# Mish as one ScalarE function, with a new order of the whole program and casts spread over three engines

## The chip, the cores and the metric

The kernel runs on one core of one Trainium2 chip. The core has a matmul engine (TensorE, PE in the profile), three engines for elementwise work (VectorE, DVE; ScalarE, ACT; GpSimd, POOL), and one queue (SyncE, SP) that issues the DMAs here. Each engine takes its instructions in the order in which the program was written and waits on semaphores for the others. The metric is the device time of one execution in microseconds; the median of three runs before is 551.99 us (550.8 to 553.58).

## The reference

Two parts follow one another. The first is a gated linear recurrence (4 batches, 8 heads, 768 steps, head size 40), the second a feed-forward layer with Mish over 3072 tokens (320 to 2048 to 320). Everything is float32.

```python
for t in range(S):                                   # first part, per batch and head
    m_new = np.maximum(f_gate[:, :, t] + m, i_gate[:, :, t])
    f_stab = np.exp(f_gate[:, :, t] + m - m_new); i_stab = np.exp(i_gate[:, :, t] - m_new); m = m_new
    C = f_stab * C + i_stab * outer(v_t, k_t);  n = f_stab * n + i_stab * k_t
    y[:, :, t] = sigmoid(o_gate_t) * (C @ q_t) / np.maximum(np.abs(n . q_t), 1.0)

h = x @ w_in                                         # second part, x = y as 3072 x 320
sp = np.where(h > 20.0, h, np.log1p(np.exp(np.minimum(h, 20.0))))
g = h * np.tanh(sp)                                  # Mish
out = g @ w_out
```

The weights w_in and w_out come as float64 and are handed to the kernel as pairs of 32-bit words.

## The kernel before

The 3072 tokens are cut into 12 units of 256 tokens (u or n), each of two chunks (c) of 128. For each chunk the first part is done in matrix form: `scores` (q against k), `decay` (four Exp passes on ACT, one for each head), `causal` (the mask, on POOL), `pmul`, `intra` and `inter` (the two parts of the output), `state_mm` and `state` (the carried matrix), `denom`, the output gate in five steps `gate_o`, `gate_den`, `xmul`, and then the transpose `flip_mm` and its two halves `flip_hi` and `flip_lo`.

The second part goes in 96 slots: 12 units times 8 pairs of hidden blocks (p). To keep float32 exactness with a faster matmul type, each operand is split into a rounded high half and the rest. A slot is `mm1` (two halves j of 8 matmuls of 256 columns each, into a PSUM bank pair h, of which there are two), Mish, the split of the result into gh and gl, and `mm2` (two halves of 6 matmuls of 320 columns each, adding into acc). The tiles e, gh and gl have two buffers each.

Mish is h·(1 − 1/(0.5·(1+e^h)² + 0.5)), with e^h cut off so that it stays finite. That is six passes over a 128x512 tile and two more for the split:

| call | engine | what | line |
|---|---|---|---|
| mish_exp | ACT | Exp of h | L1503 |
| mish_min | DVE or POOL | cut at e^20 | L1507 |
| mish_rest 0, 1, 2 | ACT | Square, Ln, Exp | L1512, L1514, L1516 |
| mish_out 0 | DVE | (1 − e)·h, after which h is free | L1521 |
| mish_out 1 | DVE or ACT | gh, the rounded copy | L1196 (the helper `copy`) |
| mish_out 2 | DVE or POOL | gl = e − gh | L1528 |

All of ACT's functions in it lie in one table set, which is loaded once at the start (L1714).

The weights are converted in the kernel as well: 16 chunks (8 of w_in, 8 of w_out) are loaded, through three buffers, and go through `conv` in six steps: a scaling on ACT (L1228), three integer steps on DVE (L1230, L1232, L1234), the rounded half wih or woh (L1196, on ACT or DVE) and the rest wil or wol (L1238, on POOL or DVE). A slot p needs the conversion of its w_in chunk for mm1 and of its w_out chunk for mm2. Units 0 and 1 run their slots in alternating halves meanwhile, and their partial sums are put aside by `dump`. While weights and first inputs are loaded, 42 `warm` matmuls on zeros run on PE.

The order of the program is not that of the loops. Each call is entered by `at` with a time, and by `after` with the calls that must come before it; `emit` puts them in order of time under those needs. The times come from a table TIMES: a start for calls of the first units, an offset within the slot (of 4.4 us) for the others, and own times for the last two units. A table 'eng' in it names the engine of each cast, split and conversion. As every engine, and the SP queue too, runs in program order, this list sets what waits behind what on each.

Of the kernel before, what the change touches and what calls it, by code (L numbers as in the profile page):

```python
# [7 lines left out]
F32 = mybir.dt.float32  # L8
# [18 lines left out]
LAG = 2  # L27
KN = H * D
VN = H * D1
E20 = 485165195.40979  # L30
# [6 lines left out]
SLOT = 4.4  # L37
NB = NU
TIMES = {'mm1': [-0.149, 0.276],
 'mish_exp': -1.727,  # L40
 'mish_min': 0.556,
 'mish_rest': [0.925, -2.788, 0.213],
 'mish_out': [1.068, 1.915, -0.004],
 'mm2': [2.849, 0.289],
 'store': [2.139, 2.543],
 'decay': [[-2.011, -0.53], [1.29, 2.675]],
 'causal': [[1.179, 0.533], [0.229, 3.083]],
 'scores': [[1.493, 2.193], [2.16, 3.297]],
 'pmul': [[0.588, 2.056], [4.029, 4.412]],
 'gate_o': [[-0.073, 0.11, 0.23, 0.764, 2.964], [2.985, 3.425, 3.545, 2.599, 5.248]],  # L50
 'weigh_v': [1.002, 3.434],
 'state_mm': [1.553, 5.355],
 'state': [1.83, 4.829],
 'inter': [-0.408, 5.492],
 'intra': [[2.475, 3.282], [5.629, 5.791]],
 'denom': [3.216, 4.039],
 'gate_den': [2.212, 6.091],
 'xmul': [3.581, 6.08],
 'flip_mm': [4.447, 7.002],
 'flip_hi': [4.544, 6.181],  # L60
 'flip_lo': [4.602, 7.365],
 'load_raw': -7.874,
 'load_ea': -7.594,
 'load_kvo': [-3.832, -3.594],
 'set_abc': -4.191,
 'carry': -6.024,
 'make_qs': -5.899,
 'split_hi': [-5.402, -5.297],
 'split_lo': [-6.621, -3.312],
 'stack': -1.727,  # L70
 'xdup': [3.631, 6.13],
 'block1': 64.45,
 'eng': {'gate_o_0_0_0': 'S',
         'gate_o_0_1_0': 'S',
         'gate_o_1_0_0': 'S',
         'gate_o_1_1_0': 'S',
         'mish_out_0_0_1': 'V',
         'mish_out_0_0_2': 'G',
         'mish_out_0_1_1': 'V',
         'mish_out_0_1_2': 'G',  # L80
         'mish_out_0_2_1': 'V',
         'mish_out_0_2_2': 'G',
         'mish_out_0_3_1': 'S',
         'mish_out_0_3_2': 'G',
         'mish_out_0_4_1': 'S',
         'mish_out_0_4_2': 'G',
         'mish_out_0_5_1': 'V',
         'mish_out_0_5_2': 'G',
         'mish_out_0_6_1': 'V',
         'mish_out_0_6_2': 'G',  # L90
         'mish_out_0_7_1': 'V',
         'mish_out_0_7_2': 'V',
         'split_hi_2_0': 'V',
         'split_hi_2_1': 'V',
         'mish_min_0_0': 'V',
         'mish_min_0_1': 'G',
         'mish_min_0_2': 'G',
         'mish_min_0_3': 'G',
         'dump_0_0': 'V',
         'dump_0_1': 'V',  # L100
         'mish_min_1_0': 'V',
         'mish_out_1_0_1': 'V',
         'mish_out_1_0_2': 'G',
         'mish_min_1_1': 'V',
         'mish_out_1_1_1': 'S',
         'mish_out_1_1_2': 'G',
         'mish_min_1_2': 'V',
         'mish_out_1_2_1': 'S',
         'mish_out_1_2_2': 'G',
         'mish_min_1_3': 'V',  # L110
         'mish_out_1_3_1': 'V',
         'mish_out_1_3_2': 'G',
         'dump_1_0': 'S',
         'dump_1_1': 'S',
         'mish_min_0_4': 'V',
         'mish_min_0_5': 'G',
         'mish_min_0_6': 'V',
         'mish_min_0_7': 'V',
         'mish_min_1_4': 'G',
         'mish_out_1_4_1': 'V',  # L120
         'mish_out_1_4_2': 'G',
         'mish_min_1_5': 'V',
         'mish_out_1_5_1': 'V',
         'mish_out_1_5_2': 'V',
         'mish_min_1_6': 'G',
         'mish_out_1_6_1': 'S',
         'mish_out_1_6_2': 'G',
         'mish_min_1_7': 'V',
         'mish_out_1_7_1': 'V',
         'mish_out_1_7_2': 'G',  # L130
         'weigh_v_0_0': 'V',
         'gate_den_0_0': 'G',
# [1773 lines left out]
```

## Time and profile before

| | |
|---|---|
| median of three runs | 551.99 us |
| the profiled execution | 554.73 us |
| its span, first to last instruction | 553.0 us |
| mean granted TensorE clock | 0.944 |
| busy: PE, DVE, ACT, POOL | 507.7, 430.8, 358.3, 212.1 us |
| matmuls | 3714 |
| first matmul of mm1 | 46.8 us |
| last output copy begins | 549.9 us |

A busy engine is one with an instruction in flight. PE's matmuls are pipelined: while it is dense, the next one begins some 0.12 us after the last although each is shown as lasting about 0.3 us, so the count of matmuls in a stretch says more than the busy share. DVE, ACT and POOL take one instruction at a time, with a small overlap. Rows of groups give the busy sum, the mean time of one in ns, and the idle time of the engine just ahead of them with what ended it.

### The profile page before, as it was taken

What the parts mean: (1) busy time and instruction counts of PE and PEld (TensorE: products, weight loads), DVE (VectorE), ACT (ScalarE), POOL (GpSimd) and SP (SyncE); (2) the same over time, 40 slices, a digit from 0 to 9 for tenths busy, and PEclk for the clock granted to TensorE, in tenths of its full rate; (3) what the DMA queues carried; (4) which work ended last, traced back from release to release, by engine and by line L of the source; (5) the groups of instructions that cost most, each with busy time, mean ns of one, the idle gap of its engine ahead of it and who ended that gap; (6) DMA issues with size and microseconds to landing.
All of it is one profiled execution on the core that took longest, in us unless ns stands there. A gap on an engine that the chain in (4) does not pass through costs nothing.

```text
span 553.0 us, 10133 instructions
## 1 busy us (share of the span) xinstructions
PE 507.7 (92%) x3714; PEld 490.9 (89%) x3714; DVE 430.8 (78%) x814; ACT 358.3 (65%) x718; POOL 212.1 (38%) x194
## 2 busy tenths in 40 slices
PE   6999877789999988998998998998998998999997
PEld 5998766778999988998998998997988997999997
DVE  7858999999977669759669769769669769778654
ACT  3636864766774756765766756756756756775774
POOL 4726986775651215116225215215215215212010
PEclk9558977997999998999998999999999999999999
DMA  7884853565434552453562552552551561510000
GB/s 204 262 250 149 268 196 105 165 194 154 143 90 137 165 148 82 148 135 111 160 166 70 158 154 81 163 162 71 166 169 58 172 182 41 170 35 1 2 25 24
DMA packets 40778, 73.72 MB, mean 133 GB/s; under 512 B 3048, under 2 KB 22440, under 8 KB 40568
## 3 DMA queue, kind: packets, MB, share of 16 engines
q1 hardware_dynamic: 40728, 73.07, 43.8%
q8 instruction: 29, 0.48, 0.4%
q14 instruction: 21, 0.17, 0.1%
HBM read 49.27 MB, written 4.13 MB: 97 GB/s over the span
## 4 chain that ended last, share of the span: by engine, by line
PE 44%; DVE 19%; DMA 15%; SPq 9%; issue 5%; ACT 4%; POOL 3%; DVEq 0%; POOLq 0%; ACTq 0%
PE h L1499 15%; SPq L1300 8%; DMA out_dram<-ob 7%; PE acc L1545 6%; PE acc L1543 5%; PE acc L1544 5%; DMA stk<-raw 5%; PE y L1386 4%; DVE gh L1196 3%; DMA raw<-in_qk_dram 3%; DVE e L1507 3%; PE s L1335 2%; PE warm L1786 2%; DVE wr L1232 2%; PE m L1397 2%
## 5 line engine op out<-in xcount | busy, mean ns | idle before, releaser
L1499 PE MATMUL h<-xh,wih 128*128 128x256 f32 x576 | 164.2, 291 | 7.1 <-DVE e L1521 7.0
L1499 PE MATMUL h<-xh,wil 128*128 128x256 f32 x576 | 154.8, 284 | 1.0 <-DVE wil L1238 1.0
L1543 PE MATMUL acc<-woh,gh 128*128 128x320 f32 x384 | 124.9, 325 | 9.1 <-DVE gh L1196 7.6
L1545 PE MATMUL acc<-woh,gl 128*128 128x320 f32 x384 | 122.0, 318 | 3.8 <-DVE gl L1528 3.3
L1544 PE MATMUL acc<-wol,gh 128*128 128x320 f32 x384 | 120.4, 313 | 2.3 <-DVE wol L1238 2.3
L1499 PEld LDWEIGHTS h<-xh,wih 128*128 128x128 f32 x576 | 112.2, 195 | 10.5 <-DVE e L1521 6.9
L1499 PEld LDWEIGHTS h<-xh,wil 128*128 128x128 f32 x576 | 111.8, 194 | 1.4 <-DVE wil L1238 1.3
L1512 ACT ACTIVATE e<-e 128x512 f32<-128x512 f32 x96 | 60.5, 630 | 80.8 <-DVE e L1507 77.4
L1499 PE MATMUL h<-xl,wih 128*128 128x256 f32 x384 | 109.7, 286 | 1.4 <-DVE xl L1473 1.4
L1503 ACT ACTIVATE e<-h 128x512 f32<-128x512 f32 x96 | 56.9, 593 | 64.2 <-PE h L1499 47.3
L1521 DVE SCALAR_TENSOR_TENSOR e<-e,h 128x512 f32<-128x512 f32 x96 | 65.5, 683 | 32.9 <-ACT e L1516 32.5
L1543 PEld LDWEIGHTS acc<-woh,gh 128*128 128x128 f32 x384 | 74.0, 193 | 10.4 <-DVE gh L1196 8.6
L1545 PEld LDWEIGHTS acc<-woh,gl 128*128 128x128 f32 x384 | 74.0, 193 | 7.1 <-DVE gl L1528 6.4
L1499 PEld LDWEIGHTS h<-xl,wih 128*128 128x128 f32 x384 | 74.8, 195 | 2.0 <-DVE xl L1473 2.0
L1322 POOL TENSOR_SCALAR_AFFINE_SELECT d<-d 128x512 f32<-128x512 f32 x48 | 36.5, 764 | 104.4 <-ACT d L1314 104.3
L1544 PEld LDWEIGHTS acc<-wol,gh 128*128 128x128 f32 x384 | 73.8, 192 | 2.5 <-DVE wol L1238 2.5
L1507 DVE TENSOR_SCALAR e<-e 128x512 f32<-128x512 f32 x90 | 52.1, 579 | 22.1 <-ACT e L1503 21.9
L1528 DVE TENSOR_TENSOR gl<-e,gh 128x512 fp32r<-128x512 f32 x80 | 61.1, 764 | 4.5 <-ACT gh L1196 0.3
L1514 ACT ACTIVATE e<-e 128x512 f32<-128x512 f32 x96 | 60.7, 632 | 2.8
L1516 ACT ACTIVATE e<-e 128x512 f32<-128x512 f32 x96 | 60.7, 632 | 2.8
L1314 ACT ACTIVATE d<-abc,cw 128x128 f32<-128x128 f32 x184 | 57.9, 391 | 0.4 <-DMA abc<-a_dram 0.4
L1444 POOL TENSOR_TENSOR sg<-sg,den 128x320 f32<-128x320 f32 x23 | 19.7, 858 | 94.5 <-DVE den L1440 44.9
(88 smaller groups left out, 825.8 us busy)
## 6 DMA issues: line engine op xcount, KB each, us to landing
stk<-raw SPq DMA_DIRECT2D x60, 240.0 KB
kvo<-in_kvo_dram SPq DMA_DIRECT2D x24, 484.0 KB
abc<-a_dram SPq DMA_DIRECT2D x11, 1024.0 KB
raw<-in_qk_dram SPq DMA_DIRECT2D x10, 720.0 KB
wr<-in_w_out_dram SPq DMA_DIRECT2D x8, 640.0 KB
stk<-raw SPq DMA_DIRECT2D x30, 160.0 KB
wr<-in_w_in_dram SPq DMA_DIRECT2D x8, 512.0 KB
out_dram<-ob SPq DMA_DIRECT2D x20, 160.0 KB
```

Source lines behind the costliest of these rows:

```text
L1314: nc.scalar.activation(out=t[:, hh, :], in_=abc_t[u, c][h][:, c * L:(c + 1) * L], func=ACTF.Exp, bias=cw[:, ch, b * H + h:b * H + h + 1],)
L1499: nc.tensor.matmul(h_t[n, p][:, j, :], l, r, start=(k == 0), stop=(k == len(ops) - 1))
L1503: nc.scalar.activation(out=e, in_=h_t[n, p].rearrange("p a t -> p (a t)"), func=ACTF.Exp)
L1507: eng("V", "mish_min", n, p).tensor_scalar(out=e, in0=e, scalar1=E20, scalar2=None, op0=ALU.min)
L1512: nc.scalar.activation(out=e, in_=e, func=ACTF.Square, bias=1.0)
L1514: nc.scalar.activation(out=e, in_=e, func=ACTF.Ln, bias=0.5, scale=0.5)
L1516: nc.scalar.activation(out=e, in_=e, func=ACTF.Exp, scale=-1.0)
L1521: nc.vector.scalar_tensor_tensor(out=g, in0=g, scalar=1.0, in1=h, op0=ALU.subtract, op1=ALU.mult, reverse0=True)
L1528: eng("V", "mish_out", "last" if n == NB - 1 else n, p, k).tensor_tensor(out=gl, in0=e_t.pop((n, p)), in1=g_t[n, p][0].bitcast(F32), op=AL ...
L1543: nc.tensor.matmul(o, gh[:, ts], woh[:, fi, :], start=(first and jj == 0), stop=False)
L1544: nc.tensor.matmul(o, gh[:, ts], wol[:, fi, :], start=False, stop=False)
L1545: nc.tensor.matmul(o, gl[:, ts], woh[:, fi, :], start=False, stop=(last and jj == 1))
```

## The change

Mish becomes one pass of ScalarE's own function, from h in PSUM to e in SBUF. That function is in a table set of its own, "mish", so a helper `table` loads the set that the next function needs, whenever the last one loaded was the other; the decay, the output gate and the gates' Exp ask for the set of before. The split is now `split_g` 0 (gh) and 1 (gl). What `mm1` waits for is the Mish pass two slots ago, where it was the product.

TIMES is gone. In its place stand a list ORDER of all 1726 calls in their order, and a table ENG of engines. The needs (`after`) are otherwise those of before; `emit` takes the place in the list where it took the time. The number of warm matmuls is the same. By ENG, 45 of the 96 gh casts are on ACT and 51 on DVE (before: 6 and 90); all 96 gl are on DVE (before: 80, and 16 on POOL); of the 16 wil and wol 10 are on DVE (before: 3). Of the other calls on the first part, some 12 each of `weigh_v`, `gate_den` and 9 of `split_lo` move from POOL to DVE, 10 of `split_hi` from DVE to ACT.

```diff
-LAG = 2
-E20 = 485165195.40979
-SLOT = 4.4
-TIMES = {'mm1': [-0.149, 0.276],
...
+EXP = "natural_log_exp_and_others"
+NW = 42
+ENG = {n: e for e, l in {
+    "S": """
+dump_0_0 dump_1_0 dump_1_1 gate_0_256_cw gate_256_768_cw gate_o_0_0_0 gate_o_1_0_0 gate_o_2_0_0 gate_o_3_0_0
+gate_o_5_1_0 gate_o_8_0_0 split_g_0_1_0 split_g_0_2_0 split_g_0_3_0 split_g_0_5_0 split_g_0_6_0 split_g_10_0_0
...
+ORDER = """
+start load_gates warm_0 load_cst warm_1 load_kvo_0_0 warm_2 load_w_in_0 warm_3 warm_4 warm_5 load_w_in_1 warm_6
...
+load_kvo_2_0 conv_i_4_0 gate_den_1_0 scores_1_1_1 split_lo_2_0 state_1_0_0 state_1_0_1 stack_2 mm1_0_0_0 decay_2_0_0
+conv_o_2_1 conv_o_2_2 mm1_0_0_1 weigh_v_2_0 decay_2_0_1 conv_o_2_3 causal_2_0_0 conv_i_3_3 mm1_0_1_0 mish_0_0
...
+gate_o_3_0_4 mm1_0_7_1 conv_o_7_5 mm1_1_4_0 flip_hi_2_0 mish_0_7 flip_lo_2_0 mm1_1_4_1 split_g_0_7_0 split_g_0_7_1
...
+gate_o_4_0_4 mm1_2_3_0 mish_2_2 mm1_2_3_1 load_raw_5 split_g_2_2_0
+mm1_2_4_0 mish_2_3 split_g_2_2_1 mm2_2_2_0 split_g_2_3_0 split_g_2_3_1 mm2_2_2_1 mm2_2_3_0 mm2_2_3_1 mm1_2_4_1
...
+    def table(which):
+
+        if f_t.get("table") != which:
+            nc.scalar.preload_act_table_set(which)
+            f_t["table"] = which
...
     def decay(u, c, hf):
         b, ch = u // UPB, (u % UPB) * CPU + c
         t = att2.tile([128, 4, L], F32, tag="d", name="d", bufs=4)
+        table(EXP)
...
-    def mish_exp(n, p):
+    def mish(n, p):
         e_t[n, p] = e = late["moe"].tile([128, 2 * U], F32, tag="e", name="e")
-        nc.scalar.activation(out=e, in_=h_t[n, p].rearrange("p a t -> p (a t)"), func=ACTF.Exp)
...
+        table("mish")
+        nc.scalar.activation(out=e, in_=h_t.pop((n, p)).rearrange("p a t -> p (a t)"), func=ACTF.Mish)
+
+    def split_g(n, p, k):
         if k == 0:
+            gh = late["moe"].tile([128, 2 * U], F32R, tag="gh", name="gh")
+            copy(eng("V", "split_g", n, p, k), gh, e_t[n, p])
+            g_t[n, p] = [gh]
         if k == 1:
             gl = late["moe"].tile([128, 2 * U], F32R, tag="gl", name="gl")
+            eng("V", "split_g", n, p, k).tensor_tensor(out=gl, in0=e_t.pop((n, p)), in1=g_t[n, p][0].bitcast(F32), op=ALU.subtract)
             g_t[n, p].append(gl)
...
+            at(mm1, n, p, j)
+            after(("mm1", n, p, 0) if j else ("flip_lo", n, 1), ("conv", "i", p, 5), ("mish", *s2))
+        at(mish, n, p)
+        after(("mm1", n, p, 1), ("split_g", *s2, 1), ("open_moe",))
+        for k in range(2):
+            at(split_g, n, p, k)
+            after(("split_g", n, p, 0) if k else ("mish", n, p), ("mm2", *s2, 1))
```

More of the change, by code (lines that the diff above doesn't have):

```diff
@@ new lines @@
+weigh_v_7_0 weigh_v_9_0
+""",
+    "G": """
+gate_0_256_c2 gate_256_768_c2
+""",
+}.items() for n in l.split()}
+ORDER = """
+start load_gates warm_0 load_cst warm_1 load_kvo_0_0 warm_2 load_w_in_0 warm_3 warm_4 warm_5 load_w_in_1 warm_6
+gate_0_256_m warm_7 gate_0_256_a warm_8 gate_0_256_b gate_0_256_a2 warm_9 load_kvo_0_1 warm_10 gate_o_0_0_0 warm_11
+load_raw_0_0 gate_o_0_0_1 warm_12 gate_o_0_0_2 warm_13 gate_256_768_m gate_o_0_0_3 gate_256_768_b warm_14 warm_15
+gate_0_256_A conv_i_0_0 warm_16 warm_17 warm_18 load_raw_0_1 warm_19 warm_20 gate_o_0_0_4 bcast_0 gate_0_256_c bcast_1
@@ L1192, in eng @@
     def eng(default, *key):
-        return engines[T["eng"].get("_".join(str(x) for x in key), default)]
+        return engines[ENG.get("_".join(str(x) for x in key), default)]
+    def table(which):
+        if f_t.get("table") != which:
+            nc.scalar.preload_act_table_set(which)
+            f_t["table"] = which
     def copy(e, out, in_):
@@ L1199, in group @@
         return min(3, H - 3 * g)
+    f_t, e_t, h_t, g_t, acc, late = {}, {}, {}, {}, {}, {}
     wraw = {}
@@ L1347, in gate_o @@
         t = sg_t[u, c]
-        act = T["eng"].get(f"gate_o_{u}_{c}_0") == "S"
+        act = ENG.get(f"gate_o_{u}_{c}_0") == "S"
+        if k in (1, 2, 4) or (k == 0 and act):
+            table(EXP)
         if k == 0 and act:
@@ L1478, in mlstm_moe_kernel, with at @@
     events = []
-    def at(t, fn, *args):
-        t = T["start"].get(name(fn, args), T["block1"] + (t - NP) * SLOT)
-        if args and args[0] in (NB - 2, NB - 1):
-            t0 = T["end"].get(name(fn, (("prev", "last")[args[0] - NB + 2],) + args[1:]))
-            t = t if t0 is None else T["block1"] + (NB - 2) * NP * SLOT + t0
-        events.append((t, len(events), fn, args, []))
-    f_t, e_t, h_t, g_t, acc, late = {}, {}, {}, {}, {}, {}
+    rank = {n: x for x, n in enumerate(ORDER.split())}
+    def at(fn, *args):
+        events.append((rank[name(fn, args)], len(events), fn, args, []))
     def mm1(n, p, j):
@@ L1555, in store @@
             ob = late["moe"].tile([128, DM], F32, tag="ob", name="ob")
-            copy(eng("V", "store", "last" if n == NB - 1 else n, t), ob, acc[n][t])
+            copy(eng("V", "store", n, t), ob, acc[n][t])
         nc.sync.dma_start(out=out[n * U + t * L:n * U + (t + 1) * L, :], in_=ob)
@@ L1752, in gate @@
             nc.sync.dma_start(out=a_dram[:, ts], in_=A[:, ts])
+        if k in ("eA", "w"):
+            table(EXP)
         if k == "eA":
@@ L1789, in set_abc0 @@
         abc_t[0, 1] = load_abc(0, L, U)
-    at(0.0, start)
-    at(0.0, load_gates)
+    at(start)
+    at(load_gates)
     after(("start",))
-    at(0.0, load_cst)
+    at(load_cst)
     after(("load_gates",))
@@ L1811, in mlstm_moe_kernel @@
             after(("bcast", h - 1))
-    for x in range(T["nw"]):
-        at(0.0, warm, x)
+    for x in range(NW):
+        at(warm, x)
         after(("warm", x - 1) if x else ("start",))
-    at(0.0, set_abc0)
+    at(set_abc0)
     after(("gate", *GT[0], "sA"))
     for k, (kind, p) in enumerate(chunks):
-        at(0.0, load_w_in if kind == "i" else load_w_out, p)
+        at(load_w_in if kind == "i" else load_w_out, p)
         after(("load_gates",))
```

1394 lines of the change are left out of this document (240 added, 1154 removed).

## The prediction

> **What bounds the kernel now.** I read the head of the page first, then the busy time of each engine in five stages, cut where the first matmul of the expert layer starts (46.8 us), where the last weight conversion ends (147.7 us), and at two output stores (199.4 and 488.8 us).
>
> ```profile
> span 553.0 us, 10133 instructions
> PE 507.7 (92%) x3714; PEld 490.9 (89%) x3714; DVE 430.8 (78%) x814; ACT 358.3 (65%) x718; POOL 212.1 (38%) x194
> ```
>
> ```profile
> 0.00:46.80 46.80, 42.06 (x203) 38.97 (x203) 32.71 (x53) 23.55 (x56) 24.80 (x29) 0.67 0.81 238
> 46.80:147.70 100.90, 83.42 (x567) 78.48 (x565) 96.54 (x147) 67.24 (x130) 71.49 (x50) 0.88 0.57 174
> 147.70:199.40 51.70, 49.44 (x385) 48.78 (x385) 37.19 (x79) 35.96 (x72) 17.77 (x18) 1.00 0.37 113
> 199.40:488.80 289.40, 271.70 (x2092) 263.92 (x2091) 222.89 (x454) 191.40 (x393) 90.81 (x92) 0.99 0.44 132
> 488.80:553.00 64.20, 61.06 (x478) 60.80 (x476) 41.44 (x85) 40.17 (x70) 7.28 (x9) 1.00 0.05 16
> ```
>
> The columns are the stretch, its length, busy time (and instructions) of PE, PEld, DVE, ACT, POOL, the granted clock, the DMA share and GB/s. PE at 92% invites the reading "nothing to gain on the other engines". But busy PE is not dense PE. Two 14 us stretches late in the kernel show what dense is, and one just ahead of them what a usual stretch is:
>
> ```profile
> 448.00:462.00 14.00, 11.61 (x90) 10.94 (x90) 10.38 (x20) 6.03 (x13) 5.45 (x5) 1.00 0.65 191
> 476.00:490.00 14.00, 14.00 (x114) 14.00 (x113) 10.33 (x22) 12.19 (x26) 2.95 (x4) 1.00 0.36 111
> 490.00:504.00 14.00, 14.00 (x114) 14.00 (x114) 12.00 (x27) 9.10 (x19) 3.03 (x4) 1.00 0.07 25
> ```
>
> Dense is 114 matmuls in 14.00 us, 0.1228 us each, in the usual mix. The stage 46.8 to 147.7 issued 567, worth 69.6 us, in 100.9 us, and DVE is busy 96.54 of it (96%): there DVE sets the pace. From 147.7 on, PE does; what it still waits for is named in the waits between 150 and 490 us:
>
> ```profile
> PEld acc L1543 <- DVE gh L1196: 8.6, 7, 1.3
> PE acc L1543 <- DVE gh L1196: 7.6, 7, 1.1
> PEld h L1499 <- DVE e L1521: 6.9, 8, 1.1
> PEld acc L1545 <- DVE gl L1528: 6.4, 12, 0.7
> ```
>
> All of them are links of the chain that the change shortens. Two rows give the ends of the accounts, the last conversion (146.4 + 1.3 = 147.7 us) and the last store copy (the last matmul ends just before it, at 549.9 us):
>
> ```profile
> L1238 DVE TENSOR_TENSOR wol<-wr,woh x2: 811/1058/1304, 88.9 to 146.4; 128x640 fp32r<-128x640 f32 x2
> L1196 DVE COPY ob<-acc x20: 478/492/494, 199.4 to 549.9; 128x320 f32<-128x320 f32 x20
> ```
>
> So 147.7 us hold 203 + 567 = 770 matmuls. The other 2944 would be 361.5 us when dense and took 549.9 − 147.7 = 402.2: a loss of 40.7 us. Tail: 3.1 us.
>
> **The change, part by part.** *One pass for six.* Prices, from the groups kept apart by shape (columns: busy us, mean ns of one, idle before):
>
> ```profile
> L1503 ACT ACTIVATE e<-h 128x512 f32<-128x512 f32 x96 | 56.9, 593 | 64.2 <-PE h L1499 47.3 <-DVE gl L1528 15.4 <-POOL gl L1528 1.1
> L1512 ACT ACTIVATE e<-e 128x512 f32<-128x512 f32 x96 | 60.5, 630 | 80.8 <-DVE e L1507 77.4 <-POOL e L1507 3.1
> L1514 ACT ACTIVATE e<-e 128x512 f32<-128x512 f32 x96 | 60.7, 632 | 2.8
> L1516 ACT ACTIVATE e<-e 128x512 f32<-128x512 f32 x96 | 60.7, 632 | 2.8
> L1507 DVE TENSOR_SCALAR e<-e 128x512 f32<-128x512 f32 x90 | 52.1, 579 | 22.1 <-ACT e L1503 21.9
> L1521 DVE SCALAR_TENSOR_TENSOR e<-e,h 128x512 f32<-128x512 f32 x96 | 65.5, 683 | 32.9 <-ACT e L1516 32.5
> ```
>
> Exp, Square and Ln cost alike, so Mish, which no row shows, is taken at 0.593 us, the row that also reads the bank h (0.632 at most by the others; below 0.593 nothing speaks for it). ACT loses 60.5 + 60.7 + 60.7 = 181.9 us, DVE 52.1 + 65.5 = 117.6. The chain from a finished h to its product shrinks from 0.593 + 0.579 + 3 × 0.63 + 0.683 = 3.75 us to 0.593, and h is free after that one pass: the waits of mm1 for L1521 must vanish.
>
> *Table loads.* Exp and Ln share a set; Mish is in its own. Following the new order through `table`, the set changes 67 times, 34 of them into Mish. The one load of before:
>
> ```profile
> L1714 ACT ACT_TABLE_LOAD x1 | 1.3, 1283 | 0.8 <-PEq L1892 0.8
> L1314 ACT ACTIVATE d<-abc,cw 128x128 f32<-128x128 f32 x184 | 57.9, 391 | 0.4 <-DMA abc<-a_dram 0.4
> L1196 ACT CAST gh<-e 128x512 fp32r<-128x512 f32 x6 | 3.7, 611 | 0.1
> ```
>
> 67 × 1.283 = 86.0 us. 45 of the gh casts are ACT's instead of 6: + 39 × 0.611 = 23.8. ACT: 358.3 − 181.9 + 86.0 + 23.8 = 286, 54% of the time below. So on average the loads lie beside PE's work; uncovered, one costs 1.283 us on PE. Bounds: nothing, or all 86.
>
> [...]
>
> *Casts and conversions.* These matter in the stage to 147.7 us. Its DVE account, from the groups of that window and the spread of single lines (min/median/max ns):
>
> ```profile
> L1234 DVE SCALAR_TENSOR_TENSOR wr<-wr 128x768 int32<-128x768 int32 (+1 forms) x16 | 22.3, 1395 | 0.1
> L1232 DVE SCALAR_TENSOR_TENSOR wr<-wr 128x768 int32<-128x768 int32 (+1 forms) x16 | 19.7, 1233 | 0.2
> L1230 DVE TENSOR_SCALAR wr<-wr 128x768 int32<-128x768 int32 (+1 forms) x16 | 11.9, 741 | 0.0
> L1521 DVE SCALAR_TENSOR_TENSOR e<-e,h 128x512 f32<-128x512 f32 x14 | 9.5, 677 | 1.1 <-ACT e L1516 0.9 <-POOL x L1453 0.2
> L1507 DVE TENSOR_SCALAR e<-e 128x512 f32<-128x512 f32 x9 | 7.3, 814 | 0.4 <-ACT e L1503 0.4
> ```
>
> ```profile
> L1196 DVE CAST gh<-e x90: 374/420/2045, 57.9 to 546.7; 128x512 fp32r<-128x512 f32 x90
> L1232 DVE SCALAR_TENSOR_TENSOR wr<-wr x16: 811/942/2109, 12.6 to 141.8; 128x768 int32<-128x768 int32 x8, 128x640 int32<-128x640 int32 x8
> L1528 DVE TENSOR_TENSOR gl<-e,gh x80: 681/693/1098, 137.9 to 547.3; 128x512 fp32r<-128x512 f32 x80
> L1528 POOL TENSOR_TENSOR gl<-e,gh x16: 1270/1396/2080, 58.9 to 538.1; 128x512 fp32r<-128x512 f32 x16
> L1238 POOL TENSOR_TENSOR wil<-wr,wih x7: 1837/2053/2689, 18.3 to 109.5; 128x768 fp32r<-128x768 f32 x7
> L1238 DVE TENSOR_TENSOR wil<-wr,wih x1: 1926/1926/1926, 126.3 to 126.3; 128x768 fp32r<-128x768 f32 x1
> ```
>
> The spread has a reason. Here POOL's and DVE's own instructions at one of the longest casts:
>
> ```profile
> 208.49 2.02 POOL L1292 TENSOR_TENSOR raw<-raw 120x768 f32<-120x768 f32 x1 [0.88 <-PE h L1499]
> 208.75 2.04 DVE L1196 CAST gh<-e 128x512 fp32r<-128x512 f32 x1
> ```
>
> A 0.42 us cast takes 2.04 while POOL works on SBUF, and ends when POOL does. So work taken off POOL also speeds up DVE. Counted in the new order up to its last conversion (11 Mish passes, 4 gh and 11 gl on DVE, 6 of 8 wil and 4 of 8 wol there too), DVE changes by: L1507 −7.3, L1521 −9.5; gh 9 casts to 4, about −3.8; gl + 9 × 0.69 = + 6.2; wil + 5 × 0.97 = + 4.9 (0.97 is wol's undisturbed 0.811 × 768/640; at its one row 1.926 it would be 9.6); wol 2 × 0.81 = + 1.6; other moves between DVE, ACT and POOL about + 1.3. Net −6.6. POOL in that stage had 24.8 + 71.5 = 96.3 us; without some 12 gl (1.4 each), 6 clamps, 5 wil and 2 wol it keeps about half. What contention costs: L1234, L1232 and L1230 hold 53.9 us, against 16 × (0.816 + 0.811 + 0.481) × 1.1 (half of them are the wider form) = 37 undisturbed; with the casts some 22 us. Half of that goes: −11. DVE: 129.3 − 6.6 − 11 = 111.7. Its idle time in the stage (147.7 − 129.3 = 18.4, of which 14.1 lies before 46.8 us, under loads at 238 GB/s) I leave. **Last conversion: 130 us.** Bounds: 113 (all contention and a third of the idle time gone) and 148 (the loads pace it, and nothing is gained).
>
> *The order.* At its last conversion the new order has issued only 667 matmuls, 103 fewer than before: expert work starts later (262 matmuls stand before and in its first mm1 call). So 12.6 us of PE work move behind the conversions, and eat most of the 17.7 us saved there. Left: 3714 − 667 = 3047 × 0.1228 = 374.2 us, plus what remains of the 40.7 us loss. The waits for L1521 go, those for gh shrink (45 casts leave DVE, and POOL disturbs less), those for gl stay as links; a part is no wait but switches between kinds of matmul. I take half, 20 us; bounds 8 and 41.
>
> **Sum:** 130 + 374 + 20 + 3 = 527 us of span. The profiled execution lasted 1.7 us longer than its span (554.73 against 553.0) and 2.7 more than the median 551.99, so the median forecast is 526 us, 0.95 of before.
>
> **Rivals.** *Faster still (20%):* DVE's contention and idle time both go and the short chain leaves PE 8 to 14 us of loss: 115 + 374 + 11 + 3 = 503, 502 as a median. For: DVE as a whole loses 117.6 of 430.8 us. Against: POOL keeps mask, queries and half of the splits.
>
> *The loads pace the start (17%):* conversions still end at 148, with fewer matmuls done: 148 + 374 + 20 + 3 = 545, 544. For: 238 GB/s and a DMA share of 0.81 up to 46.8 us. Against: 0.57 after it.
>
> *ACT's loads stall PE (13%; slower or even):* h has two banks, so PE can cover 28 matmuls, 3.4 us, from the end of one mm1 pair to the one that needs its bank. If an attention piece cuts in: 2 × 1.283 + 4 × 0.391 + 0.593 = 4.7 us, 1.3 exposed, on 34 returns 44 us. With 10 us of other losses: 130 + 374 + 10 + 44 + 3 = 561, 560 as a median, slower. It decides from 36/34 = 1.06 us exposed per return. For: ACT runs in its order. Against: four d buffers let decays run early, at ACT's 54%. [...]
>
> *Mish is no single pass:* were it twice the price, + 57 us on ACT, it would still be covered; inside the first case.
>
> **How the numbers follow.** Forecast 526 with its own spread of 512 to 538: 50%. With the rivals: faster by over 0.5% (about what a measurement here tells from no change) 0.50 + 0.20 + 0.17 = 0.87; the last rival is split into 0.04 within 0.5% and 0.09 slower. The range leaves out the lower half of the fast case and most of the slow one: 507 to 548.
>
> **What would show it.** Right: last conversion near 130 us; mean of the conversion lines L1230 to L1234 (by their after-numbers) well below 1.2 us; no PE wait for the Mish tile's predecessor; stretches of 112 to 114 matmuls in 14 us from there on; 68 table loads at 1.28 us. Wrong: table loads above 1.3 us or gaps around them, mm1 waiting for ACT, conversions ending at 145 with DVE idle for weights, or stretches of 90 to 100 matmuls as before.

## The result and the profile after

The changed kernel takes 531.79 us (median of four runs, 531.28 to 534.0) against 552.64 for four runs of the kernel before on the same chip: a ratio of 0.9634, with a 95% interval of 0.9596 to 0.9673. The forecast was 526, in a range of 507 to 548. The profiled execution lasted 534.0 us and its span was 532.3.

First the head of the changed kernel's page, then the busy time of its engines in three stages. They are cut where the first matmul of mm1 starts (62.5 us), where the last conversion ends (133.7 us) and at the last matmul (529.1 us). The columns are those of the stages shown of before.

```profile
span 532.3 us, 9593 instructions
PE 500.5 (94%) x3714; PEld 488.7 (92%) x3714; DVE 329.4 (62%) x646; ACT 302.0 (57%) x538; POOL 119.0 (22%) x129
```

```profile
0.00:62.50 62.50, 52.38 (x254) 48.21 (x254) 45.20 (x81) 30.13 (x67) 28.74 (x29) 0.64 0.90 239
62.50:133.70 71.20, 60.49 (x418) 58.87 (x418) 65.79 (x107) 53.46 (x88) 21.63 (x19) 0.89 0.73 196
133.70:529.10 395.40, 387.60 (x3046) 381.64 (x3044) 217.87 (x459) 218.43 (x384) 68.58 (x82) 1.00 0.38 112
```

Read them as the prediction read those of before. The start ends at 133.7 us with 254 + 418 = 672 matmuls issued. The other 3042 would take 373.6 us at 0.1228 us each and took 395.4: a loss of 21.8 us. After the last matmul come 3.2 us. So the 20.7 us of span that were gained are 14.0 of an earlier last conversion, minus 12.0 for the 98 matmuls that are no longer done by then, plus 18.9 of loss that is gone after it (40.7 − 21.8), with a tenth lost at the tail.

Next, groups of instructions on the lines of the change (busy us, mean ns of one, idle time of the engine just before and what ended it), with shapes kept apart:

```profile
L337 ACT ACT_TABLE_LOAD x68 | 87.2, 1283 | 2.0 <-PEq L1013 0.8
L650 ACT ACTIVATE e<-h 128x512 f32<-128x512 f32 x96 | 57.1, 598 | 100.2 <-PE h L645 84.9 <-DVE gl L659 9.3 <-issue 2.5
L341 ACT CAST gh<-e 128x512 fp32r<-128x512 f32 x45 | 27.7, 620 | 10.4 <-PE acc L675 9.6
L341 ACT CAST raw<-raw 120x768 fp32r<-120x768 f32 x12 | 9.7, 831 | 5.0 <-DMA ea<-ea_dram 3.0 <-DMA raw<-in_qk_dram 2.0
```

The Mish pass costs 598 ns (593 were forecast), and each of the 68 loads costs 1283 ns, as the one of before did. A stretch of ACT's timeline shows two of these loads from both sides (start us, duration us, engine, line, what):

```profile
104.39 0.80 ACT L374 ACTIVATE wr<-wr 128x640 f32<-128x640 f32 x1
105.21 1.28 ACT L337 ACT_TABLE_LOAD   x1
106.50 1.10 ACT L650 ACTIVATE e<-h 128x512 f32<-128x512 f32 x2
107.50 1.13 ACT L341 CAST gh<-e 128x512 fp32r<-128x512 f32 x2
108.66 1.28 ACT L337 ACT_TABLE_LOAD   x1
109.95 1.28 ACT L461 ACTIVATE d<-abc,cw 128x128 f32<-128x128 f32 x4
```

A load begins 0.02 to 0.03 us after the instruction ahead of it ends, and the next begins 0.01 us after the load. No further time for a switch is to be seen, except that the overlap of some 0.1 us that two of ACT's instructions in a row have (the cast starts at 107.50, the two passes ahead of it end at 106.50 + 1.10) is lost at a load.

The integer steps of the conversions, by groups on DVE up to the last conversion, and the last halves of the conversions on DVE by single lines (min/median/max ns, first and last start):

```profile
L380 DVE SCALAR_TENSOR_TENSOR wr<-wr 128x768 int32<-128x768 int32 (+1 forms) x16 | 16.0, 1008 | 0.3
L378 DVE SCALAR_TENSOR_TENSOR wr<-wr 128x768 int32<-128x768 int32 (+1 forms) x16 | 14.9, 931 | 0.8
L376 DVE TENSOR_SCALAR wr<-wr 128x768 int32<-128x768 int32 (+1 forms) x16 | 8.3, 517 | 0.0
```

```profile
L384 DVE TENSOR_TENSOR wol<-wr,woh x4: 774/816/2109, 51.6 to 132.9; 128x640 fp32r<-128x640 f32 x4
```

The means of the three steps (of the third, second and first, in the order of the rows) fell from 1395, 1233 and 741 ns to 1008, 931 and 517, their sum from 53.9 to 39.2 us. Last, PE's waits between 150 and 490 us, as shown of before (total us, times, longest):

```profile
PEld acc L676 <- DVE gl L659: 7.2, 11, 1.9
PE acc L676 <- DVE gl L659: 4.6, 7, 1.6
...
PE acc L674 <- DVE gh L341: 0.9, 1, 0.9
```

The wait for gh fell from 7.6 to 0.9 us, that of mm1 for the Mish tile's predecessor is gone from the list, and the one for gl stays.

### The profile page after: what moved, and what is told of

It reads as the page before. It is cut to its first block, busy times and chain, and to the rows that moved or that the text cites. A ratio compares the mean times of both kernels' runs of the same rounds, so it can differ in the third digit from the quotient of the medians.

```text
span 532.3 us, 9593 instructions
## 1 busy us (share of the span) xinstructions
PE 500.5 (94%) x3714; PEld 488.7 (92%) x3714; DVE 329.4 (62%) x646; ACT 302.0 (57%) x538; POOL 119.0 (22%) x129
## 4 chain that ended last, share of the span: by engine, by line
PE 63%; DVE 13%; DMA 12%; ACT 5%; SPq 3%; issue 3%; POOL 1%; DVEq 0%; ACTq 0%; POOLq 0%
PE h L645 25%; PE acc L676 9%; PE acc L674 8%; PE acc L675 8%; PE y L535 6%; PE s L482 3%; DVE gl L659 3%; DMA ea<-ea_dram 3%; DMA abc<-a_dram 3%; DMA raw<-in_qk_dram 2%; DMA wr<-in_w_in_dram 2%; PE m L546 2%; SPq L446 2%; PE y L525 2%; DMA kvo<-in_kvo_dram 1%
## 5 line engine op out<-in xcount | busy, mean ns | idle before, releaser
L645 PE MATMUL h<-xh,wih 128*128 128x256 f32 x576 | 161.6, 290 | 0.2 <-ACT e L650 0.2
L674 PE MATMUL acc<-woh,gh 128*128 128x320 f32 x384 | 120.4, 313 | 2.8 <-ACT gh L341 1.9
L675 PE MATMUL acc<-wol,gh 128*128 128x320 f32 x384 | 118.7, 309 | 0.0
L645 PEld LDWEIGHTS h<-xh,wih 128*128 128x128 f32 x576 | 111.7, 194 | 0.9 <-ACT e L650 0.6
L659 DVE TENSOR_TENSOR gl<-e,gh 128x512 fp32r<-128x512 f32 x96 | 74.7, 780 | 39.5 <-ACT gh L341 35.8
L337 ACT ACT_TABLE_LOAD x68 | 87.2, 1283 | 2.0 <-PEq L1013 0.8
L676 PEld LDWEIGHTS acc<-woh,gl 128*128 128x128 f32 x384 | 72.4, 189 | 11.8 <-DVE gl L659 10.6
L341 DVE CAST gh<-e 128x512 fp32r<-128x512 f32 x51 | 25.2, 495 | 53.7 <-ACT e L650 44.8
L535 PE MATMUL y<-kvo,d 128*128 128x41 f32 x384 | 51.4, 297 | 1.8 <-DVE d L487 1.5
L535 PEld LDWEIGHTS y<-kvo,d 128*128 128x128 f32 x384 | 49.9, 209 | 2.8 <-DVE d L487 2.0
L487 DVE TENSOR_TENSOR d<-s,d 128x512 f32<-128x512 f32 x48 | 32.2, 683 | 15.1 <-PE s L482 11.0
L341 ACT CAST gh<-e 128x512 fp32r<-128x512 f32 x45 | 27.7, 620 | 10.4 <-PE acc L675 9.6
```

The lines of the kernel that those rows point to most:

```text
L337: nc.scalar.preload_act_table_set(which)
L341: (e.copy if e is nc.scalar else e.tensor_copy)(out=out, in_=in_)
L487: nc.vector.tensor_tensor(out=p, in0=s_t.pop((u, c, hf)), in1=p, op=ALU.mult)
L535: nc.tensor.matmul(y_t[u, c][:, h * D1:(h + 1) * D1], p[:, hh, :], kvo_t[u, c][:, KN + h * D1:KN + (h + 1) * D1], start=(ch == 0 and h == ...
L645: nc.tensor.matmul(h_t[n, p][:, j, :], l, r, start=(k == 0), stop=(k == len(ops) - 1))
L659: eng("V", "split_g", n, p, k).tensor_tensor(out=gl, in0=e_t.pop((n, p)), in1=g_t[n, p][0].bitcast(F32), op=ALU.subtract)
```

## The experiments

Each ratio is against the kernel before, measured beside it, whose medians lay between 553.8 and 555.3 us; the changed kernel's own ratio is 0.9634. The times named "loss" are worked out as above, with 0.1228 us for each matmul behind the last conversion.

### What the table loads cost

Without any switch: the pass becomes Exp, which is in the set of the decays.

```diff
-        table("mish")
-        nc.scalar.activation(out=e, in_=..., func=ACTF.Mish)
+        table(EXP)
+        nc.scalar.activation(out=e, in_=..., func=ACTF.Exp)
```

> The changed kernel with Exp in place of Mish, so that ACT's table set never changes: the 67 table loads (86 us of ACT) are gone, every other instruction stays where it is. What is computed is e^h in place of Mish(h). Forecast (the loads lie beside PE's work): 526 to 533 us, against 531.8 with them. Rival (ACT's loads stall PE): each of 34 returns to Mish had exposed some time; at the 1.3 us worked out there it would now be 490, at half a microsecond 515.

With every switch doubled, by a load of a third set ahead of it:

```diff
         if f_t.get("table") != which:
+            if "table" in f_t:
+                nc.scalar.preload_act_table_set("gelu_and_others")
             nc.scalar.preload_act_table_set(which)
```

> The changed kernel with one more table load (of a third set) ahead of each of the 67: ACT's busy time goes from 302 to 388 us. Forecast (the loads are covered by the two banks of h and by the order): less than 20 us more, 535 to 550. Rival (they stall PE): 34 returns with two more loads of 1.283 us each, 87 us more, near 619.

Without loads: 528.53 us, ratio 0.954 (0.9493 to 0.9587). With twice as many: 581.78 us, ratio 1.0485 (1.0421 to 1.055). Stages of the kernel without loads, cut at its last conversion:

```profile
0.00:131.30 131.30, 109.45 (x670) 103.97 (x671) 110.26 (x187) 67.36 (x143) 51.88 (x47) 0.78 0.82 220
131.30:522.50 391.20, 385.28 (x3046) 380.04 (x3045) 218.44 (x460) 147.72 (x329) 68.51 (x82) 1.00 0.39 114
```

The same of the one with twice as many, and its longest waits of PE's weight loads over the whole span:

```profile
0.00:144.70 144.70, 113.75 (x679) 107.24 (x680) 109.38 (x187) 98.52 (x167) 49.43 (x47) 0.78 0.74 200
144.70:578.20 433.50, 404.57 (x3037) 392.32 (x3035) 215.20 (x460) 287.47 (x439) 67.37 (x82) 0.97 0.35 102
```

```profile
PEld acc L678 <- DVE gl L661: 16.7, 26, 4.0
PEld h L647 <- ACT e L652: 16.4, 13, 4.1
```

The 67 loads hold 86 us of ACT and cost 3.3 us by the medians, 5.2 by the two ratios: some 0.05 to 0.08 us for each load. The next 67 of the same length cost 50 us, far more than the 20 at most that the forecast allowed, of which 11 lie in the start and 39 behind it, and PE's weight loads now wait 16.4 us for the Mish pass, in the changed kernel 0.6. Some 12 of the 39 behind the start are lost by the granted clock: it was 0.5 in 27.3 us there, which is 13.7 us of full rate, against 1.7 in the changed kernel. So a pause of PE was paid twice there. The cover of the loads is there, and it is nearly used up. The rival that lets ACT's loads stall PE had the right mechanism and the wrong place: per return to Mish the kernel exposes 0.1 to 0.15 us where that rival needed 1.06, and the doubled loads expose 50/34 = 1.5.

### What paces the start

Two suspects were taken away, first each alone. The three integer steps on DVE are the largest block of its time there; two of them are left out:

```diff
-        if k == 2:
+        if k == 99:
...
-        if k == 3:
+        if k == 98:
```

> The changed kernel without the second and third integer step of each weight conversion, so that the converted weights are wrong: some 30 us of DVE's work before the last conversion are gone, the loads stay. If DVE paces the stage (forecast): the last conversion comes at 105 to 115 us in place of 133.7 and the time falls to 508 to 515. If the loads pace it (rival): last conversion after 125 us, and 525 or more.

The weights' transfers are the other: only the first three of the 16 chunks are loaded, the rest are converted from what lies in the three buffers.

```diff
+        t = wbuf[k % WB].rearrange("p (k f w) -> p k f w", k=3, w=2)
...
+        if k < WB:
             nc.sync.dma_start(out=tf[:, 0:2], in_=src[0:256].rearrange("(k p) f -> p k f", p=128))
```

> The changed kernel with only the first 3 of 16 weight chunks loaded; the other 13 are converted from what lies in the three buffers (so the weights are wrong): DVE's work stays, 8.7 MB of loads in the first 130 us are gone. If DVE paces the stage (forecast): last conversion at 125 to 134 us, 523 to 532 us in all. If the loads pace it (rival): last conversion at 105 to 118 us, 505 to 518 in all.

Without the integer steps: ratio 0.9566 (0.9478 to 0.9655), by single executions from 527.37 to 536.37 us (the profile is of one of 536.29). Without the transfers: 534.33 us, ratio 0.9633 (0.9573 to 0.9693). Neither can be told from the changed kernel, and the forecast of 508 to 515 us for the first, with DVE as what paces the stage, failed. Stages of the first, cut about where the changed kernel's are, and then of the second:

```profile
0.00:62.00 62.00, 49.12 (x251) 45.20 (x252) 32.41 (x67) 29.23 (x66) 23.60 (x29) 0.65 0.92 237
62.00:133.60 71.60, 61.53 (x419) 59.83 (x419) 46.37 (x87) 54.22 (x89) 21.09 (x19) 0.87 0.72 199
```

```profile
0.00:62.00 62.00, 51.31 (x240) 47.15 (x240) 42.16 (x77) 30.08 (x67) 26.45 (x29) 0.60 0.65 170
62.00:133.60 71.60, 60.46 (x409) 58.62 (x409) 68.17 (x106) 51.83 (x86) 24.56 (x20) 0.87 0.44 127
```

And their last conversions, as shown of the changed kernel above, in the same order:

```profile
L384 DVE TENSOR_TENSOR wol<-wr,woh x4: 774/818/1202, 50.0 to 132.7; 128x640 fp32r<-128x640 f32 x4
```

```profile
L388 DVE TENSOR_TENSOR wol<-wbuf,woh x4: 769/818/2486, 54.6 to 135.6; 128x640 fp32r<-128x640 f32 x4
```

In the first, DVE is busy 78.8 us where it was 111.0 up to the last conversion, and this conversion started at 132.7 instead of 132.9 us (forecast: done at 105 to 115). In the second, the DMA share fell from 0.90 to 0.65 and from 0.73 to 0.44, and it started at 135.6. Each suspect might have been hidden by the other, so both were taken away at once (the two diffs together).

> The changed kernel without the second and third integer step and with only 3 of 16 weight chunks loaded (the weights are wrong). Each of the two alone left the last conversion where it was (133.6 and 136.4 us against 133.7). If the two are parallel paths of equal length: last conversion at 108 to 120 us, 505 to 520 in all. If a third thing paces the stage (the units' own chain on PE at half clock, or ACT): 125 to 135 us again, 522 to 534 in all.

Measured: 524.48 us, ratio 0.9455 (0.9402 to 0.9507). Its last conversion ended at 127.1 us, 6.6 us earlier, and the loss behind it was 20.1. Its stages, and pieces of its chain of waits that ended last (start us, us, what):

```profile
0.00:62.00 62.00, 51.20 (x259) 47.27 (x260) 36.57 (x74) 31.01 (x71) 26.13 (x30) 0.65 0.70 190
62.00:133.60 71.60, 66.12 (x464) 65.09 (x464) 48.05 (x90) 55.84 (x91) 19.71 (x18) 0.87 0.40 112
```

```profile
57.25 4.51 POOL raw L442 x2
...
65.77 1.78 SPq L450
...
70.54 4.44 DMA stk<-raw
```

So in the changed kernel DVE and the transfers were each covered by the other, but only for about 7 us. Below both lies a third path of nearly the same length. In its chain stand the first units' own work, POOL's making of queries and SP's issues of the stacking (62 to 70 us). Which of these it is, no run of its own tells; that stays open.

### What the single pass is worth without the order, and the order without it

The order, engines and slots of before, with the one pass in place of the six:

```diff
+        table("mish")
+        nc.scalar.activation(out=e, in_=h_t.pop((n, p)).rearrange("p a t -> p (a t)"), func=ACTF.Mish)
...
     def mish_min(n, p):
+        pass
...
     def mish_rest(n, p, k):
+        pass
```

> The kernel of before, its order and engines kept, with Mish in one pass (no cut, no Square, Ln and second Exp, no product) and the helper that loads the table set: in this order the set changes 123 times, 158 us of ACT. If the single pass is what brings the gain, whatever the order (rival): 520 to 535 us. If one pass pays only in an order that keeps the loads few and ahead of time (what the doubled loads point to): 540 to 560, no clear gain over before.

The order and engines of after, with all six passes in the one call:

```diff
-        table("mish")
-        nc.scalar.activation(out=e, in_=h, func=ACTF.Mish)
+        nc.scalar.activation(out=e, in_=h, func=ACTF.Exp)
+        nc.vector.tensor_scalar(out=e, in0=e, scalar1=485165195.40979, scalar2=None, op0=ALU.min)
+        nc.scalar.activation(out=e, in_=e, func=ACTF.Square, bias=1.0)
+        nc.scalar.activation(out=e, in_=e, func=ACTF.Ln, bias=0.5, scale=0.5)
+        nc.scalar.activation(out=e, in_=e, func=ACTF.Exp, scale=-1.0)
+        nc.vector.scalar_tensor_tensor(out=e, in0=e, scalar=1.0, in1=h, op0=ALU.subtract, op1=ALU.mult, reverse0=True)
```

> The changed kernel, its order and engines kept, with Mish in the six passes of before, all at the place where the one pass stands, the cut and the product on DVE: one table load in all. The chain from h to its product is 3.75 us again, and ACT and DVE wait for one another in it. Theory: slower than before, 570 to 620 us. Rival (the order and the spread of casts alone bring the gain): 535 to 550.

The old order once more, with Exp as the one pass, so that it has no switches either (the order of before needs 124 loads with Mish):

```diff
-        table("mish")
-        nc.scalar.activation(out=e, in_=..., func=ACTF.Mish)
+        table(EXP)
+        nc.scalar.activation(out=e, in_=..., func=ACTF.Exp)
```

> The kernel of before with one pass for Mish in its old order (552.3 us, 124 table loads), now with Exp in the place of Mish, so that the set never changes; what is computed is e^h in place of Mish(h). If the table loads ate the gain of the single pass there: 525 to 538 us. If the old order cannot use a shorter chain (PE's calls and the conversions stand where the long chain put them): 545 to 553.

| | six passes | one pass |
|---|---|---|
| order and engines of before | 1 | 0.9964 (0.9933 to 0.9995); without switches 0.9934 (0.9886 to 0.9983) |
| order and engines of after | 1.4524 (1.4457 to 1.4591) | 0.9634 (0.9596 to 0.9673) |

Neither half of the change is worth much by itself: the pass alone brings less than 1%, the order alone, with the six passes in one call, costs 45% (an order that spreads the six calls was not run). The loads are not what holds up the old order: without any of them it gains some 2 us more, and the two intervals overlap.

The pass alone does end the conversions earlier. Their last one in the old order with Mish:

```profile
L1248 DVE TENSOR_TENSOR wol<-wr,woh x2: 1279/1592/1906, 84.1 to 141.5; 128x640 fp32r<-128x640 f32 x2
```

It takes 1.28 us and ends at 142.8, 4.9 us before that of the kernel before, with 771 matmuls done against 770. But the loss behind it is 43.3 us against 40.7, so less than half of this is left at the end.

What holds the old order up behind the conversions is read from two things. First, PE's longest wait between 150 and 490 us in the old order with Mish, and POOL's and DVE's instructions at one of its long casts:

```profile
PE acc L1547 <- DVE gh L1206: 11.0, 7, 1.9
```

```profile
288.27 1.99 POOL L1302 TENSOR_TENSOR raw<-raw 120x768 f32<-120x768 f32 x1 [0.55 <-PE y L1399]
...
288.53 2.02 DVE L1206 CAST gh<-e 128x512 fp32r<-128x512 f32 x1
```

The wait of mm1 for the product has gone from the list, as forecast, but the wait for gh grew from 7.6 us to 11.0 (10.1 without switches). A gh cast that falls on one of POOL's makings of queries takes 2.02 us, and PE pauses for it, once in each unit, whatever stands ahead of it in the chain: between 150 and 490 us there are seven such casts of 2.0 us in the kernel before, seven in the old order with Mish and seven in that without switches. Second, the stages behind the start. For 150 to 525 us, the kernel before, then the old order with Mish, then that without switches, then the changed kernel:

```profile
150.00:525.00 375.00, 355.04 (x2745) 346.59 (x2744) 284.75 (x584) 249.37 (x501) 111.04 (x113) 0.99 0.39 118
```

```profile
150.00:525.00 375.00, 360.05 (x2746) 356.63 (x2746) 209.45 (x433) 247.32 (x375) 104.83 (x110) 0.96 0.40 119
```

```profile
150.00:525.00 375.00, 359.58 (x2769) 356.04 (x2769) 209.29 (x433) 111.84 (x274) 106.77 (x110) 0.97 0.41 119
```

```profile
150.00:525.00 375.00, 367.20 (x2890) 361.50 (x2889) 210.01 (x443) 209.28 (x366) 67.95 (x81) 1.00 0.40 116
```

The single pass did take waits off PE: its weight loads (PEld) are idle for 18.4 us in the old order, for 28.4 in the kernel before. But it issued no more matmuls (2746 against 2745), and the granted clock is the column that changed, from 0.99 to 0.96. In slices of 2 us around the pause shown:

```profile
288.00:290.00 2.00, 0.75 (x7) 0.60 (x6) 2.00 (x3) 0.00 (x0) 1.73 (x1) 1.00 1.09 377
290.00:292.00 2.00, 0.92 (x4) 0.66 (x5) 1.97 (x4) 0.30 (x1) 1.04 (x2) 1.00 0.77 286
292.00:294.00 2.00, 2.00 (x12) 2.00 (x11) 0.43 (x3) 1.97 (x3) 1.35 (x2) 0.66 0.00 0
294.00:296.00 2.00, 2.00 (x11) 2.00 (x10) 1.35 (x4) 1.83 (x3) 0.43 (x3) 0.50 0.02 4
```

PE is idle for 2.3 of 4 us, and then works for 3.4 us at a granted clock of 0.5, with a matmul of mm1 every 0.21 us in place of 0.115. Between 150 and 525 us such stretches cost, by the granted clock, 15.0 us of full rate in the old order with Mish and 11.9 without switches (seven and seven of them behind the start, one in each unit), 3.4 in the kernel before (two) and 1.7 in the changed kernel (one). In the old order with one pass PE's pause in each unit is one of 1.0 to 1.9 us, most often with another of 0.5 right behind it; in the kernel before it is one of 1.1 and 0.5, with some 0.5 to 0.8 taken four us earlier, and five of seven go by without a drop. So the shorter chain took waits away and drew what was left together, and the clock took back what had been gained. An account of the same 375 us shows it (us; the first column is 375.00 less 0.1228 for each matmul issued):

| | loss | weight loads idle | lost by the clock | left over |
|---|---|---|---|---|
| kernel before | 37.9 | 28.4 | 3.4 | 6.1 |
| old order, Mish | 37.8 | 18.4 | 15.0 | 4.4 |
| old order, no switches | 35.0 | 19.0 | 11.9 | 4.1 |
| changed kernel | 20.1 | 13.5 | 1.7 | 4.9 |

The clock's 11.6 us more eat the 10.0 us that the waits lost. That the drops follow the pauses is read from the times; no run keeps the pauses and the clock apart.

The waits of the six passes in the new order:

```profile
DVE e L655 <- ACT e L654: 192.0, 95, 2.0
...
PEld h L645 <- DVE e L655: 36.0, 20, 2.7
```

The kernel lost 804.98 − 531.79 = 273 us, 2.85 for each of the 96 slots, where 570 to 620 us in all had been expected. The chain from h to the product is 3.75 − 0.60 = 3.15 us longer. The new order asks for the product right behind the Mish call, so the length of the chain lies open. How much of the 273 us is the chain itself isn't separated: the granted clock, 0.809 in the mean against 0.939, makes up to some 121 us of it by an estimate from these means and the two spans.

### What the spread over three engines is worth

The gh casts back on DVE, but for the six that were ACT's before:

```diff
+ENG.update({n: 'V' for n in ENG if n.startswith('split_g')})
+ENG.update({n: 'S' for n in ['split_g_0_3_0', 'split_g_0_4_0', 'split_g_1_1_0', 'split_g_1_2_0', 'split_g_1_6_0', 'split_g_11_5_0']})
```

> The changed kernel with the gh casts on the engines of before: 90 on DVE and 6 on ACT in place of 51 and 45. DVE gets 39 casts of 0.42 to 0.50 us, ACT loses 39 of 0.62. Theory of the prediction (the spread takes waits for gh and gl off PE): 3 to 10 us slower than the change, 535 to 542. Rival (DVE at 62% has room, and a cast is faster there): 528 to 533.

And the 16 gl and 13 wil and wol back on POOL:

```diff
+ENG.update({f'split_g_{x}_1': 'G' for x in ['0_0', '0_1', ...]})
+ENG.update({f'conv_{k}_{p}_5': 'G' for k in 'io' for p in range(8) if (k, p) not in (('o', 3), ('i', 7), ('o', 7))})
```

> The changed kernel with the 16 gl and 13 of the 16 wil and wol on POOL again, as before: POOL gets some 35 us more work, nearly all before the last conversion, DVE some 17 us less. Theory of the prediction (POOL's work slows DVE's casts, and that matters): 536 to 545 us, the three integer steps slower again. Rival (the stage is paced by something else): 528 to 535.

With gh on DVE: 540.99 us, ratio 0.977 (0.971 to 0.983), last conversion 136.9 us, loss 25.9. With POOL as before: 541.78 us, ratio 0.9773 (0.9727 to 0.9818). Its start, up to its last conversion:

```profile
0.00:141.80 141.80, 115.30 (x666) 108.10 (x667) 111.43 (x167) 83.87 (x155) 78.03 (x66) 0.75 0.75 204
```

POOL is busy 78.0 us in it where the changed kernel had 28.7 + 21.6 = 50.4, and 21 of DVE's instructions of about 0.8 us there, some 17 us, are POOL's again (167 against 188). Yet DVE is busy 111.4 us, as it was with that work (111.0): what it no longer does, its other instructions lose by being slower beside POOL. Of the three integer steps the first and the second are slower again (687 and 1354 ns in the mean, against 517 and 931), the third is not (984 against 1008). The conversions end 8 us later. The loss behind them is 20.6 us, unchanged, so POOL's part of the gain lies in the start, and that of the gh casts in both. With the gh casts on DVE again, their durations there are these:

```profile
L345 DVE CAST gh<-e x90: 409/426/1755, 70.2 to 532.7; 128x512 fp32r<-128x512 f32 x90
```

None takes the 2.0 us of the kernel before; in the changed kernel the longest takes 2.11. So it isn't the move of these casts to ACT that keeps them off POOL's makings of queries.

### The warm matmuls

PE shows a granted clock of 0.5 from 17.0 to 68.2 us in the changed kernel (before: 13.8 to 44.5 us), although warm matmuls run there. Two runs changed these: no warm matmuls at all, or each as two bf16 matmuls of 256 columns.

```diff
     def warm(...):
+        return
```

> The changed kernel without its 42 warm calls (84 matmuls of 0.213 us in the first 55 us, at half clock nearly all the time). If PE's own order paces the start, with the warm matmuls in it: first mm1 up to 10 us earlier than 62.5 us, and 522 to 528 in all. If they fill only waits: 529 to 535; if they keep the clock up for what follows: later than that.

```diff
-        nc.tensor.matmul(f_t["warm"], z[:, 0:128], z[:, 0:128], start=True, stop=True)
+        for r in range(2):
+            nc.tensor.matmul(f_t["warm"], z[:, 0:128], z, start=True, stop=True)
```

> The changed kernel with each warm call as two bf16 matmuls of 256 columns on the same zeros, in place of one float32 matmul of 128: about the same time on PE, other work in the array. If the granted clock of the first 68 us depends on the kind of matmul: above 0.64 in the first 62.5 us, and 522 to 530 in all, since the units' own matmuls there take 0.11 us in place of 0.21. If not: clock and time as in the change, 530 to 534.

As bf16: 532.51 us, ratio 0.9612 (0.9564 to 0.966), clock 0.5 from 11.7 to 66.3 us but for some 3 us at 29. Between these two kinds there is no difference in time. Without warm matmuls three executions took 530.17, 532.58 and 535.76 us (the ratio of these is 0.9619, 0.9548 to 0.9689): no time was lost. The fourth, the profiled one, took 1046.74 us. Its granted clock and its largest group on PE:

```profile
core 0: 1045.0 us, clock 1.000
```

```profile
L645 PE MATMUL h<-xh,wih 128*128 128x256 f32 x576 | 279.1, 487 | 0.0
```

The same group has 290 ns as its mean in the changed kernel. The whole execution ran at half of the usual rate or below, and no change of the clock is recorded in it. The last section comes back to it.

## Why the prediction was right, and which steps were not

**The sum.** It was 130 + 374 + 20 + 3 = 527 us of span; measured were 133.7 + 373.6 + 21.8 + 3.2 = 532.3. The order's own cost, expert work that moves behind the conversions, was taken at 103 matmuls and came out at 98. Of the 5 us that the forecast was short, 3.7 are in the last conversion and 1.8 in the loss. That the sum came out so close is in part luck, since two of its terms had the wrong reason.

**The last conversion: the DVE account.** DVE's busy time up to it was forecast at 111.7 us and measured at 45.2 + 65.8 = 111.0. Its idle time, which was left at 18.4, is 22.7: that is the size that was off. The contention behind the −11 us is shown from both sides, by the three means above and by the run with POOL as before. It was sized too low: the three integer steps alone lost 14.7 us, and DVE's other changes came to −3.6 in place of −6.6.

**"There DVE sets the pace" did not hold for the changed kernel.** With 32 us of DVE's work left out, the last conversion did not move. Without the transfers it came 2.7 us later, and without both 6.6 us earlier. The term came out right because the engine that was counted is one of at least three nearly equal strands, which is luck as far as the method goes. For the kernel before, of which the sentence spoke, no such run was made. The old order with one pass is the nearest: DVE is busy for 120.3 us up to the last conversion there, against 129.3, and it ends 4.9 us earlier, so DVE's work had a part. For the rival "The loads pace the start" the same holds from the other side: the transfers alone pace nothing there.

**"All of them are links of the chain that the change shortens" was the step that failed.** The chain did get shorter, and the wait of mm1 for L1521 vanished. But with the single pass alone, in the old order, the loss behind the conversions stayed (43.3, and 39.4 without switches, against 40.7). The wait for gh isn't set by the chain's length but by a cast that POOL holds up: it grew from 7.6 to 11.0 us. With the other waits gone it became one longer pause in each unit, behind which the clock dropped. The prediction had no term for the clock behind the start: it read 1.00, 0.99 and 1.00 there and took it as given. In the changed kernel the wait and the drops went away with the new list and the moves between engines together. Of the 19 us gained there, the gh casts on ACT bring 4.1 (25.9 against 21.8), and the 16 gl and 13 conversions taken off POOL bring none. The rest belongs to the list itself or to the other moves from POOL to DVE and ACT; no run separates these. One of them also took the gh casts off POOL's makings of queries, since at most one cast of 2 us is left between 150 and 490 us with 90 of them on DVE, and with POOL's splits and conversions as before. So the size, half of 40.7, held by luck, without its reason; that POOL disturbs less stood in it as an aside only. The switches between kinds of matmul, which the prediction counts in the loss without a size, are seen as small: between 470 and 515 us in the kernel before, the first matmul of mm1 or mm2 behind a piece of the first part is followed by the next after 0.17 to 0.24 us, where 0.12 to 0.15 is usual, some 0.05 to 0.1 us for each switch.

**The table loads.** Their number, their length and their cover were forecast as they came: 68, 1.283 us, and 3 to 5 us of 86 exposed. The rival with ACT's stalls fell on its own bound, by 0.1 to 0.15 us exposed for each return where 1.06 decides. The run with doubled loads shows that it was a close rival all the same: with 2 × 1.283 us for each switch the kernel is slower than before.

**ACT's sum.** It was 286 us and is 302.0. Some 4 us of the difference are other moves: the casts of the row of 831 ns above, twelve instead of two, are 8.1 us more and were in the text on the change but not in the sum, and fewer casts of xh and of wih take 5.2 off. The other 12 us are overlap. ACT's groups add up to 377.9 us in the kernel before and to 309.5 in the changed one, 19.6 and 7.5 us more than it is busy, since instructions in a row overlap by some 0.1 us. The prediction took three passes off at their full length, and with them went overlap that it hadn't counted. It cost next to nothing, since ACT is covered.

**Other signs.** The forecast named stretches of 112 to 114 matmuls in 14 us from the last conversion on. Two stretches of the changed kernel, one of each sort:

```profile
210.00:224.00 14.00, 12.75 (x94) 12.23 (x93) 8.59 (x10) 7.30 (x12) 6.92 (x4) 1.00 0.61 173
252.00:266.00 14.00, 14.00 (x116) 13.90 (x115) 7.11 (x15) 8.65 (x16) 1.94 (x4) 1.00 0.71 182
```

Some stretches with 87 to 94 remain, so the loss of 21.8 us is not spread evenly; in the first of these POOL is busy more than three times as long as in the second. Two of its gl subtractions (median 0.69 us in the kernel before) take 2.14 and 2.32 us there, each begun 0.3 us behind a making of queries on POOL, and PE is idle for 1.05 us at the second. So part of what is left of the loss has the cause that the gh casts had.

## What to carry to other kernels

When one engine is dense behind a start-up, a forecast can be made of the time at which the start ends, the instructions left by then at the rate of a stretch without waits, and a loss that is read from the waits. Here it came within about 1%, although the reasons for two terms were wrong, so test the reasons apart from the sum. Taking passes out of a chain is worth little until the order and the spread over engines use the shorter chain: ask of each wait what makes its last link slow, and read the granted clock beside the waits, since here a drop to 0.5 for 3.4 us behind a pause of 1.0 to 1.9 us cost 1.7 us of full rate more. To learn what paces a stage, take away two suspects together and not only each alone; and where work is hidden, double it once, since here the first 86 us were all but free (3.3 to 5.2 us) and the next 86 cost 50.

## What the runs showed of the hardware

An execution of the kernel without warm matmuls ran slowly from beginning to end (1046.74 us against 530.17 to 535.76 of the other three; 487 ns for the matmul that has 290 otherwise) with a granted clock recorded as 1.000. From 60 to 540 us it issued 86 to 103 matmuls in each 30 us and then up to 1020 us 114 to 128, where the dense rate is 244. PE was slow and ACT was not: ACT's busy time was 304.5 us, in the changed kernel 302.0. The other three show mean clocks of 0.984 to 0.990, the changed kernel 0.935 to 0.945 although they take as long, so the mean clock of a run without warm matmuls can't be set beside that of one with them. None of the other executions on record, all with warm matmuls, was slow in this way. One in four is too few to say how often this happens, and no run shows that warm matmuls always prevent it; that they cost no time here is shown (531.28 to 534.0 us with them, 530.17 to 535.76 in the three executions without).

Behind the start the clock fell to 0.5 for 3.4 us after PE had been idle for 1.6 to 2.3 us of 4, in every unit of the old order with Mish as one pass. The pause's length alone doesn't decide: in the changed kernel one of 1.6 us went by without a drop, and one of 1.04 us had one behind it. The drops lie on a grid: in each of four traces (before, changed, old order with Mish and without switches) any two begin a whole multiple of 3.413 us apart, as 207.30, 248.26 and 292.63 us in the old order with Mish (12 and 13 times).

The clock of 0.5 in the start lasts 51 us in the changed kernel (17.0 to 68.2) and 31 in the one before (13.8 to 44.5), although PE is busy for 52.4 of the first 62.5 us of the changed kernel.

A table load took its 1283 ns, with 0.01 to 0.03 us on each side, where ACT worked without a break (104 to 111 us in the changed kernel), and it took away the overlap of some 0.1 us that two instructions in a row have there.

Beside POOL, DVE's gh casts, gl subtractions and integer steps slowed down: a gh cast took 2.02 us in place of 0.42, a gl subtraction 2.32 in place of 0.69, and the second integer step 1354 ns in the mean in place of 931 with POOL's work as before. So 17 us of work moved to POOL left DVE's busy time up to the last conversion unchanged (111.4 us against 111.0). The long cast shown of the old order with Mish starts 0.26 us behind POOL's instruction and ends 0.29 us behind that one's end.
